# One score tensor of five banks for two heads, and a third bank for the other products, in a thresholded-attention and feed-forward kernel

## The chip, the cores and the metric

The kernel runs on one core of one Trainium2 chip. The metric is the time of the whole kernel on the device, in microseconds; before the change it is 1397.89 us (median of three runs, 1397.81 to 1398.3).

## What is computed

Two blocks follow each other, for a batch of 8 sequences of 576 tokens. The first is attention over 8 heads of 64 features, in which a weight is kept only where the score comes within tau of the row's largest score:

```python
scores = scale * np.matmul(q, k.transpose(0, 1, 3, 2))
thresh = np.max(scores, axis=-1, keepdims=True) - tau
scores = np.where(scores >= thresh, scores, -1000000000.0)
scores = scores - np.max(scores, axis=-1, keepdims=True)
attn = np.exp(scores)
attn = attn / (np.sum(attn, axis=-1, keepdims=True) + 1e-09)
return np.matmul(attn, v).astype(np.float32)
```

The heads' outputs are put side by side into rows x of 512 features. The second block normalizes each row and puts it through two layers with 2048 hidden features:

```python
xn = (x - mu) / np.sqrt(var + 1e-06) * g_ln
ch = np.maximum(xn @ w_ch1, 0.0) @ w_ch2
return (x + ch).astype(np.float32)
```

q, k, v and tau are fp32; the weights of the second block can come as 64-bit floats, and are then converted on the chip in the first part of the run.

## The kernel before

**Steps.** The work is cut into 72 steps, nine to a batch (`SLOTS`). A step handles a pair of heads and 256 query rows: steps 0 to 3 the first 256 rows of the four pairs of heads, steps 5 to 8 the second half's, and step 4 (`s == HP`) the 64 rows that are left over, of all pairs at once. Each step has four blocks of 128 rows by 576 scores, two to a head.

**Scores** (`scores`, L373 to L394). A head has 64 features, so its matmuls use 64 of TensorE's 128 rows; head 0 uses the upper half, head 1 the lower, and both run at the same time. Each head has a PSUM tensor of its own of three banks of 512 fp32 columns (L361). Its two blocks begin at column 128 (`FREE`) and end at 1280, and `span` (L366) cuts them at bank borders into pieces of 384, 192, 320 and 256 columns. The pieces are sorted so that the heads take turns. An fp32 matmul shows as two records in the profile, a pass each.

**What reads the scores.** `exponentials` (L396): VectorE takes the row maxima of a head's two blocks in one reduction (L404, one for each head), GpSimd makes the thresholds of them (L408), ScalarE takes the four exponentials (L415), two before the step's first quarter of other work and two after it. `weights` (L417): VectorE multiplies each block by its mask and sums the rows (L422), takes the reciprocals (L427, in batch 0 L429), and GpSimd divides (L438). In batch 0 the division is instead part of a product with a diagonal matrix.

**Weights times v.** The weights are turned, from batch 1 on by VectorE's block transposes (L504, L498) and a round trip through DRAM (scr, then em and rest, issued on SyncE's queue), in batch 0 by TensorE (`turn_weights`, tiles tp and tr). One step later `values_of` (L532) multiplies them by v (L550); ScalarE copies the result to x (L567, L558). Before the change the result lies in `pv_behind`: the 256 columns behind head 0's scores, in the same bank as the end of these scores. Only in steps 0 to 4 of batch 0 it takes a tile of the pool `ps_ff` instead.

**The other products.** Everything else on TensorE (tp and tr; the mean; p1, the first layer; var; p2 and seg, the second layer) takes one bank at a time of the pool `ps_ff`, which has two banks in turn (L76). ScalarE empties most of them (L472, L487, L729, L812), VectorE the mean, in the centring (L599). The second layer's products are done in seven segments, with sums and differences on VectorE and GpSimd (L797, L816, L824).

**Order.** Each engine runs its instructions in the order in which the program issues them. The loop at L949 issues a step: first its scores, then the reductions and the first two exponentials, then four quarters of other work: `second_part` deals out pieces of the two layers by a planned share, `turn` prepares the next q and k on VectorE (L341 to L351, in steps 8, 0, 1 and 2), small calls that have been put off run between, and at set quarters of the next step the turned weights are fetched and multiplied by v. In batch 0 and the start of batch 1, `conversion.tick()` puts the conversion of weights between, most of it on VectorE (L269 to L296). The framework itself adds the waits between engines, from what each instruction reads and writes.

Of the kernel before, what the change touches and what calls it, by code (L numbers as in the profile page):

```python
# [8 lines left out]
F32 = mybir.dt.float32  # L9
# [9 lines left out]
def kernel(  # L19
# [31 lines left out]
    nc = tc.nc  # L51
    B, H, S, D = q.shape
# [3 lines left out]
    HP = H // 2  # L56
# [5 lines left out]
    QH = 256  # L62
# [9 lines left out]
    small = ctx.enter_context(tc.tile_pool(name="small", bufs=4))  # L72
    dram = ctx.enter_context(tc.tile_pool(name="dram", bufs=3, space=bass.MemoryType.DRAM))
    ffn = ctx.enter_context(tc.tile_pool(name="ffn", bufs=2))
    ps_sc = ctx.enter_context(tc.tile_pool(name="ps_sc", bufs=1, space=bass.MemoryType.PSUM))
    ps_ff = ctx.enter_context(tc.tile_pool(name="ps_ff", bufs=2, space=bass.MemoryType.PSUM))  # L76

    tau_sb = consts.tile([128, 1], F32, name="tau_sb")
    scl_sb = consts.tile([128, 1], F32, name="scl_sb")
# [278 lines left out]


    FREE = 128  # L360
    sc = [ps_sc.tile([128, 3 * 512], F32, name=f"sc{i}") for i in range(2)]  # L361
    pv_behind = sc[0][:, FREE + 2 * S : FREE + 2 * S + QH]
    pairs = [t[:, FREE : FREE + 2 * S].rearrange("p (j n) -> p j n", j=2) for t in sc]
    blocks = [pairs[i // 2][:, i % 2] for i in range(4)]

    def span(at, n):  # L366

        while n:
            m = min(n, 512 - at % 512)
            yield at, m  # L370
            at, n = at + m, n - m

    def scores(b, s):  # L373


        hp, half = (s, 0) if s < HP else (s - HP - 1, 1)

        pieces = []
        for h in range(2):
            t = 0  # L380
            for j in range(2):
                first = FREE + j * S
                for at, n in span(first, S):
                    pieces.append((t, h, j, at, n, at - first))
                    t += n
        for t, h, j, at, n, o in sorted(pieces):
            r = slice(64 * h, 64 * h + 64)
            for i in range(2 if s == HP else 1):
                qT, kT, ql = turned[b * HP + (2 * j + i if s == HP else hp)]
                nc.tensor.matmul(  # L390
                    sc[h][64 * i : 64 * i + 64 if s == HP else 128, at : at + n],
                    lhsT=ql[r] if s == HP else qT[r, half, j * 128 : (j + 1) * 128],
                    rhs=kT[r, o : o + n], start=True, stop=True,
                )  # L394

    def exponentials(n):  # L396


        neg = small.tile([128, 4], F32, tag="neg", name="neg")
        thr = small.tile([128, 4], F32, tag="thr", name="thr")  # L400
        es = e_room[(n + 1) % 2 if n < SLOTS else 0]
        for h in range(2):
            i = slice(2 * h, 2 * h + 2)
            nc.vector.tensor_reduce(  # L404
                out=neg[:, i], in_=pairs[h],
                axis=AXL.X, op=ALU.max, negate=True,
            )
            nc.gpsimd.tensor_scalar(  # L408
                out=thr[:, i], in0=neg[:, i], scalar1=-1.0, scalar2=low_sb,
                op0=ALU.mult, op1=ALU.add,  # L410
            )
        for i in range(4):
            if i == 2:
                yield es, thr
            nc.scalar.activation(es[:, i], blocks[i], func=AF.Exp, bias=neg[:, i : i + 1])  # L415
# [111 lines left out]
    def x_of(g):  # L527
        if g not in groups:
            groups[g] = ffn.tile([128, NK, TOK], F32, tag="x", bufs=3, name="x")
        return groups[g]  # L530

    def values_of(b, s, turned_weights):  # L532

        em, er = turned_weights
        pv = pv_behind
        if b == 0 and s <= HP:
            pv = ps_ff.tile([128, QH], F32, tag="ff", name="pv")
        if s == HP:
            outs = [(hp, pv[:, hp * 64 : hp * 64 + 64]) for hp in range(HP)]
            pick = lambda t, hp, h: t[  # L540
                :, hp % 2 * 2 : hp % 2 * 2 + 2, (2 * h + hp // 2) * 32 : (2 * h + hp // 2) * 32 + 32
            ]
        else:
            outs = [(s if s < HP else s - HP - 1, pv)]
            pick = lambda t, hp, h: t[:, :, 64 * h : 64 * h + 64]
        for hp, dst in outs:
            vt, vr = values_in[b * HP + hp]
            for c in range(J + 1):
                for h in range(2):
                    nc.tensor.matmul(  # L550
                        dst[64 * h : 64 * h + 64],
                        lhsT=vt[:, h, c, :] if c < J else vr[:, h, :],
                        rhs=pick(em[:, :, c] if c < J else er, hp, h),
                        start=(c == 0), stop=(c == J),
                    )
        if s == HP:
            for t in range(2):
                nc.scalar.copy(  # L558
                    x_of(2 * b + t)[:, :, QH:],
                    pv.rearrange("p (u t x) -> p t u x", u=HP, t=2)[:, t],  # L560
                )
                for c in range(1, NK):
                    add_feature(2 * b + t, c, slice(QH, TOK))
        else:
            g = 2 * b + (s > HP)
            hp = outs[0][0]
            nc.scalar.copy(x_of(g)[:, hp, :QH], pv)  # L567
            if hp:
                add_feature(g, hp, slice(0, QH))

    def add_feature(g, c, cols):

        x = groups[g]
        if g not in sums:
            sums[g] = ffn.tile([128, TOK], F32, tag="sum", bufs=2, name="sum")
        nc.gpsimd.tensor_tensor(  # L576
            out=sums[g][:, cols], in0=x[:, 0, cols] if c == 1 else sums[g][:, cols],
            in1=x[:, c, cols], op=ALU.add,
        )
# [369 lines left out]
    for n in range(NS):  # L949
        b, s = divmod(n, SLOTS)  # L950
        ticks = (1, 3, 4)[: 2 + n // 3] if n < 6 else range(1, 7)

        def tick(i):
            if i in ticks:
                conversion.tick()

        scores(b, s)
        run(n, -1)
        rest = exponentials(n)
# [34 lines left out]
        else:  # L994
# [9 lines left out]
        at_quarter(  # L1004
            n + 1, 1 if b == 0 and s <= HP else 3,
            lambda b=b, s=s, box=box: values_of(b, s, box[0]),
        )
        if s in (HP, 2 * HP):
# [52 lines left out]
```

## Time and profile before

| | |
|---|---|
| median of three runs | 1397.89 us |
| the profiled execution | 1397.5 us |
| its span, first to last instruction | 1395.7 us |
| TensorE (PE) busy | 1337.3 us, 96% |
| VectorE (DVE) busy | 931.2 us, 67% |
| GpSimd (POOL) busy | 609.7 us, 44% |
| ScalarE (ACT) busy | 460.4 us, 33% |
| granted TensorE clock | 0.993 |
| one batch from the third on | 160.60 us |
| scores (L390), products with v (L550) on the chain that ended last | 10% and 10% of the span |

Times are in microseconds from the span's start. A row of the view in order of time gives the start, the length, the engine, the line, the operation, what it writes and reads, its shape, and how many instructions were merged in it; in brackets stands how long the engine had been idle, and which instruction it waited for. A row of the list of waits gives who waited for whom, the total, the number of times and the longest. Busy time of matmuls comes from modelled ends, so a busy TensorE is not TensorE at its peak.

### The profile page before, as it was taken

The page shows a single profiled execution, that of the slowest core. Times are in us where ns is not written, and L with a number is a line of the kernel's source. Part 1 is how long each engine was busy: PE and PEld are TensorE (multiplying, and loading weights), DVE is VectorE, ACT ScalarE, POOL GpSimd, SP SyncE. Part 2 cuts the span into 40 slices and gives each one's busy share as a digit, 9 for nine tenths or more (in the row PEclk, how much of TensorE's full clock was granted, in tenths as well). Part 3 has the DMA queues.
Part 4 walks back from the last instruction along what each step waited for, and adds up shares of the span by engine and source line. Part 5 has one row for each costly group of instructions (what it writes and reads, how often), then busy time and mean ns, then how long its engine had stood idle before and what let it go on. Part 6 is the DMA issues. An engine that isn't in the chain of part 4 may idle for free.

```text
span 1395.7 us, 35606 instructions
## 1 busy us (share of the span) xinstructions
PE 1337.3 (96%) x15048; PEld 986.9 (71%) x15048; DVE 931.2 (67%) x1638; ACT 460.4 (33%) x923; POOL 609.7 (44%) x809
## 2 busy tenths in 40 slices
PE   4888999999999999999999999999999999999996
PEld 3665665867768596877869586776858677685966
DVE  5998967676776767657776767657775767766211
ACT  3877613232332323232232323323232323323120
POOL 2444444544433454343444455353444444334413
PEclk8999999999999999999999999999999999999998
DMA  9722355447744476446754477445764476443211
GB/s 231 175 77 70 95 145 153 154 146 187 196 133 159 136 191 180 142 137 185 192 160 146 150 196 188 138 148 151 187 180 143 134 183 184 127 161 129 63 18 18
DMA packets 316383, 205.48 MB, mean 147 GB/s; under 512 B 242368, under 2 KB 273856, under 8 KB 308160
## 3 DMA queue, kind: packets, MB, share of 16 engines
q1 hardware_dynamic: 311456, 202.62, 50.8%
q8 instruction: 118, 1.93, 0.6%
q10 hardware_dynamic: 4736, 0.59, 0.4%
q14 instruction: 41, 0.34, 0.1%
q0 software_dynamic: 32, 0.00, 0.0%
HBM read 119.41 MB, written 83.76 MB: 146 GB/s over the span
## 4 chain that ended last, share of the span: by engine, by line
PE 89%; DVE 5%; ACT 2%; issue 1%; POOL 0%; POOLq 0%; DVEq 0%; ACTq 0%
PE p L101 36%; PE seg L101 30%; PE sc L550 10%; PE sc L390 10%; DVE e L422 1%; PE tp L101 1%; DVE neg L404 1%; PE var L101 0%; PE mean L101 0%; DVE w L269 0%; ACT e L415 0%; PE tr L478 0%; ACT part L812 0%; DVE hidden L296 0%; DVE w L296 0%
## 5 line engine op out<-in xcount | busy, mean ns | idle before, releaser
L101 PE MATMUL p<-xc,w 128*64 128x288 f32 x4096 | 518.1, 408 | 13.0 <-ACT hidden L729 5.5
L101 PEld LDWEIGHTS p<-xc,w 128*64 128x64 f32 x4096 | 288.9, 137 | 224.6 <-ACT hidden L729 16.0
L404 DVE TENSOR_REDUCE neg<-sc 128x2 f32<-128x1152 f32 x144 | 188.8, 1352 | 271.1 <-PE sc L390 271.0
L415 ACT ACTIVATE e<-sc,neg 128x576 f32<-128x576 f32 x288 | 196.8, 744 | 247.7 <-DVE neg L404 247.7
L438 POOL TENSOR_SCALAR e<-e,den 128x576 f32<-128x576 f32 x252 | 194.1, 783 | 134.5 <-DVE den L427 134.3
L101 PE MATMUL seg<-hidden,w 128*64 128x144 f32 x3840 | 248.0, 287 | 0.0
L101 PEld LDWEIGHTS seg<-hidden,w 128*64 128x64 f32 x3840 | 235.1, 137 | 11.6 <-issue 7.7
L422 DVE SCALAR_TENSOR_TENSOR e<-sc,thr,e 128x576 f32<-128x576 f32 x288 | 222.0, 810 | 13.9 <-ACT e L415 13.2
L729 ACT ACTIVATE hidden<-p 128x288 f32<-128x288 f32 x256 | 105.9, 414 | 241.0 <-PE p L101 239.2
L408 POOL TENSOR_SCALAR thr<-neg,low_sb 128x2 f32<-128x2 f32 x144 | 42.5, 295 | 306.1 <-DVE neg L404 302.1
L390 PE MATMUL sc<-kT,qT 64*128 64x384 f32 (+3 forms) x1024 | 150.6, 425 | 20.1 <-DVE qT L350 10.1
L504 DVE STREAM_TRANSPOSE et<-e 128x1152 f32<-128x1152 f32 x112 | 153.1, 1374 | 14.8 <-POOL e L438 14.0
L390 PEld LDWEIGHTS sc<-kT,qT 64*128 64x128 f32 x1024 | 94.3, 191 | 69.9 <-issue 18.2
L550 PE MATMUL sc<-em,v_in 128*64 128x256 f32 (+1 forms) x1408 | 130.8, 329 | 0.0
L101 PE MATMUL seg<-hidden,stage 128*64 128x144 f32 x1920 | 123.1, 286 | 0.0
L101 PEld LDWEIGHTS seg<-hidden,stage 128*64 128x64 f32 x1920 | 117.9, 137 | 3.5 <-issue 2.3
L550 PEld LDWEIGHTS sc<-em,v_in 128*64 128x64 f32 x1408 | 86.4, 137 | 32.2
L797 POOL TENSOR_TENSOR hidden<-hidden 128x576 f32<-128x576 f32 x60 | 84.4, 1426 | 27.3 <-ACT hidden L729 19.0
L576 POOL TENSOR_TENSOR sum<-sum,x 128x256 f32<-128x256 f32 (+1 forms) x64 | 32.6, 509 | 113.2 <-ACT x L567 110.7
L797 DVE TENSOR_TENSOR hidden<-hidden 128x576 f32<-128x576 f32 x60 | 49.1, 853 | 47.8 <-PE seg L101 38.1
L567 ACT COPY x<-sc 128x256 f32<-128x256 f32 x60 | 22.3, 372 | 164.7 <-PE sc L550 115.3
L812 ACT COPY part<-seg 128x288 f32<-128x288 f32 x75 | 30.1, 401 | 131.2 <-PE seg L101 109.6
(151 smaller groups left out, 1186.6 us busy)
## 6 DMA issues: line engine op xcount, KB each, us to landing
scr<-et SPq DMA_DIRECT2D x63, 1152.0 KB, 4.9
em<-scr SPq DMA_DIRECT2D x63, 1024.0 KB, 5.9
out_dram<-ot SPq DMA_DIRECT2D x256, 36.0 KB, 4.9
q_in<-in_q_dram SPq DMA_DIRECT2D x124, 72.0 KB, 2.7
k_in<-in_k_dram SPq DMA_DIRECT2D x120, 72.0 KB, 3.0
rest<-scr SPq DMA_DIRECT2D x63, 128.0 KB, 6.0
v_in<-in_v_dram SPq DMA_DIRECT2D x28, 256.0 KB, 5.2
w<-in_moe_w_ch_dram SPq DMA_DIRECT2D x10, 512.0 KB, 6.2
```

What stands on the lines that cost most here:

```text
L101: nc.tensor.matmul(out[r], lhsT=lhsT[:, r], rhs=rhs, **flags)
L390: nc.tensor.matmul(sc[h][64 * i : 64 * i + 64 if s == HP else 128, at : at + n], lhsT=ql[r] if s == HP else qT[r, half, j * 128 : (j + 1) ...
L404: nc.vector.tensor_reduce(out=neg[:, i], in_=pairs[h], axis=AXL.X, op=ALU.max, negate=True,)
L408: nc.gpsimd.tensor_scalar(out=thr[:, i], in0=neg[:, i], scalar1=-1.0, scalar2=low_sb, op0=ALU.mult, op1=ALU.add,)
L415: nc.scalar.activation(es[:, i], blocks[i], func=AF.Exp, bias=neg[:, i : i + 1])
L422: nc.vector.scalar_tensor_tensor(out=es[:, i], in0=blocks[i], scalar=thr[:, i : i + 1], in1=es[:, i], op0=ALU.is_ge, op1=ALU.mult, accum_o ...
L438: nc.gpsimd.tensor_scalar(out=es[:, i], in0=es[:, i], scalar1=den[:, i : i + 1], scalar2=1.0, op0=ALU.mult, op1=ALU.mult,)
L504: nc.vector.transpose(et[:, :, 64 * h : 64 * h + 64].rearrange("p n (j c) -> p j n c", j=2), es[:, 2 * h : 2 * h + 2].rearrange("p j (n c) ...
L550: nc.tensor.matmul(dst[64 * h : 64 * h + 64], lhsT=vt[:, h, c, :] if c < J else vr[:, h, :], rhs=pick(em[:, :, c] if c < J else er, hp, h) ...
L576: nc.gpsimd.tensor_tensor(out=sums[g][:, cols], in0=x[:, 0, cols] if c == 1 else sums[g][:, cols], in1=x[:, c, cols], op=ALU.add,)
L729: nc.scalar.activation(hidden[:, d], p1, func=AF.Relu)
L797: eng.tensor_tensor(out=out[at], in0=in0[at], in1=in1[at], op=op)
```

## The change

Both heads' scores go into one PSUM tensor of five banks. Head 0 keeps columns 128 to 1280; head 1 follows directly, from 1280 to 2432. The third bank (columns 1024 to 1536, `BOTH`) so holds the end of head 0's scores and the start of head 1's. Head 1's pieces are cut at other places than before: 256, 320, 192 and 384 columns. In the sorted order head 1's piece in the shared bank is the second to be issued, and head 0's is the last.

[...] Therefore, after head 1's piece, VectorE copies one column of it to a small tile (`mark`), and head 0's piece in the same bank is made to wait for that copy by hand.

The bank that becomes free goes to `ps_ff`, which now has three in turn, and the products with v always take one of these; `pv_behind` is gone.

```diff
-    ps_ff = ctx.enter_context(tc.tile_pool(name="ps_ff", bufs=2, space=bass.MemoryType.PSUM))
+    ps_ff = ctx.enter_context(tc.tile_pool(name="ps_ff", bufs=3, space=bass.MemoryType.PSUM))
...
-    sc = [ps_sc.tile([128, 3 * 512], F32, name=f"sc{i}") for i in range(2)]
-    pv_behind = sc[0][:, FREE + 2 * S : FREE + 2 * S + QH]
-    pairs = [t[:, FREE : FREE + 2 * S].rearrange("p (j n) -> p j n", j=2) for t in sc]
+    sc = ps_sc.tile([128, 5 * 512], F32, name="sc")
+    BOTH = (FREE + 2 * S) // 512
+    in_order = mybir.DependencyInfo(mybir.DependencyClass.Sync, mybir.DependencyReason.DATA)
+    starts = [FREE, FREE + 2 * S]
+    pairs = [sc[:, at : at + 2 * S].rearrange("p (j n) -> p j n", j=2) for at in starts]
...
-                first = FREE + j * S
+                first = starts[h] + j * S
...
-                nc.tensor.matmul(
-                    sc[h][64 * i : 64 * i + 64 if s == HP else 128, at : at + n],
+                mm = nc.tensor.matmul(
+                    sc[64 * i : 64 * i + 64 if s == HP else 128, at : at + n],
...
+                if h == 0 and at // 512 == BOTH:
+                    tc.add_manual_dep(mm.ins, seen.ins.name, in_order, reason="same bank")
+            if h == 1 and at // 512 == BOTH:
+                mark = small.tile([128, 1], F32, tag="mark", name="mark")
+                seen = nc.vector.tensor_copy(mark, sc[:, at : at + 1])
...
-        pv = pv_behind
-        if b == 0 and s <= HP:
-            pv = ps_ff.tile([128, QH], F32, tag="ff", name="pv")
+        pv = ps_ff.tile([128, QH], F32, tag="ff", name="pv")
```

## The prediction, made before the result was known

> **What bounds the kernel now.** I read the page first (busy shares, chain), then a table of one stretch per batch, the list of waits, and then instructions in order of time around two steps. TensorE is nearly always busy, and from 330 us on each batch of nine steps repeats the last one exactly; here are the busy shares of the page and, from the table by stretches, one such batch (length, then busy time of PE, PEld, DVE, ACT, POOL, granted clock, DMA share, GB/s):
>
> ```profile
> PE 1337.3 (96%) x15048; PEld 986.9 (71%) x15048; DVE 931.2 (67%) x1638; ACT 460.4 (33%) x923; POOL 609.7 (44%) x809
> ...
> 651.70:812.30 160.60, 159.97 (x1826) 118.43 (x1824) 109.37 (x195) 47.51 (x96) 72.46 (x101) 1.00 0.57 163
> ```
>
> PE is idle for 0.63 us of 160.60. So every microsecond that TensorE waits in these batches is a microsecond of the total, and hardly any wait is left to be won. The list of waits says what there is:
>
> ```profile
> DVE neg L404 <- PE sc L390: 271.0, 64, 7.6
> ACT e L415 <- DVE neg L404: 247.7, 65, 6.4
> ...
> PE sc L390 <- DVE e L422: 11.1, 9, 7.2
> ...
> PE p L101 <- ACT hidden L729: 5.5, 3, 2.8
> PE p L101 <- ACT part L812: 4.6, 8, 0.6
> ```
>
> VectorE waits for scores (271 us in 64 waits), and that is slack. TensorE's waits for a bank to be emptied by ScalarE (5.5 and 4.6 us, and in the first 100 us some 11.7 us of tp and tr for em) are all that a third bank can give back. One step in order of time (batch 4, step 3):
>
> ```profile
> 705.83 2.21 PE L390 MATMUL sc<-kT,qT 64*128 64x384 f32 x16
> ...
> 707.37 0.48 DVE L643 STREAM_TRANSPOSE ot<-y 128x288 f32<-128x288 f32 x1 [0.79 <-POOL y L816]
> ...
> 708.14 2.62 DVE L404 TENSOR_REDUCE neg<-sc 128x2 f32<-128x1152 f32 x2 [0.29 <-PE sc L390]
> 709.59 1.37 ACT L415 ACTIVATE e<-sc,neg 128x576 f32<-128x576 f32 x2 [3.23 <-DVE neg L404]
> ...
> 710.86 0.41 ACT L729 ACTIVATE hidden<-p 128x288 f32<-128x288 f32 x1
> ...
> 711.07 0.82 DVE L422 SCALAR_TENSOR_TENSOR e<-sc,thr,e 128x576 f32<-128x576 f32 x1 [0.31 <-ACT e L415]
> 711.15 1.38 ACT L415 ACTIVATE e<-sc,neg 128x576 f32<-128x576 f32 x2
> ```
>
> Call the start of the scores S (705.83). VectorE ends its earlier work 2.02 us after S; the reduces follow at S+2.31; ScalarE's first two exponentials start as soon as the first head's reduce is over, beside the second reduce; the first masking product (L422) needs two exponentials, not four.
>
> Two more places show how accesses to one PSUM tensor are ordered:
>
> ```profile
> 71.50 0.79 DVE L422 SCALAR_TENSOR_TENSOR e<-sc,thr,e 128x576 f32<-128x576 f32 x1
> ...
> 72.22 0.80 DVE L422 SCALAR_TENSOR_TENSOR e<-sc,thr,e 128x576 f32<-128x576 f32 x1
> ...
> 73.09 0.91 PE L390 MATMUL sc<-kT,qT 64*128 64x384 f32 x2 [0.42 <-DVE e L422]
> ...
> 687.17 0.37 ACT L567 COPY x<-sc 128x256 f32<-128x256 f32 x1 [5.43 <-DVE y L816]
> 687.80 1.81 PEld L390 LDWEIGHTS sc<-kT,qT 64*128 64x128 f32 x16 [0.20 <-ACT x L567]
> ```
>
> The first score piece goes to columns 128 to 512, bank 0 of the first tensor. At 73.09 it is released by the second masking product, which reads banks 1 and 2, not by the first, which reads bank 0 and ended 0.7 us before; at 687.80 by a copy out of bank 2. I take it that all accesses of different engines to one PSUM tensor run in the order of the program, whatever their banks. This is the choice that the forecast hangs on.
>
> [...]
>
> **The change, part by part.**
>
> *The mark, VectorE free.* The pieces now run head 0 (384 columns), head 1 (256, shared bank), the mark, then six more. The wait written out is for head 0's last piece only; by the order above already the third piece (head 1, 320) waits for the mark, since it writes the same tensor. Scores cost 0.83 ns per column and pass, two passes, the heads side by side: 2 x 1152 x 0.83 + 0.11 at the front = 2.04 us to the last column. Head 1's first piece is done at 0.11 + 2 x 0.21 + 0.17 (a 256-column record lasts 0.384 us, 0.21 of it columns) = 0.70. VectorE starts 0.10 later (reduce against the end of the scores, 705.83 + 2.21 to 708.14). The mark is not in the trace; the nearest row is a reciprocal of 128x2 at 0.166 us, with 0.08 (accumulator read, 128x1) and 0.30 as bounds: 0.17. To TensorE 0.05 (73.04 to 73.09). It resumes at 1.02; head 1 has 896 columns left, 1.49 + 0.11, so the end is 2.62 in place of 2.04: **+0.58 us a step**, bounds 0.4 to 0.9. All later matmuls queue behind it, so nothing covers it. The uneven pairs of pieces (up to 0.1 us) lie inside this.
>
> *The mark, VectorE late.* If VectorE ends its work P after S, the mark starts at P+0.06, TensorE resumes at P+0.28 and ends at P+1.88: the cost is P - 0.16. Last VectorE instruction against S in a steady batch, read as above for steps 0 to 8: -3.8, -3.4, -0.6, +2.0, -2.2, -1.4, -4.4, -5.2, +1.0.
>
> *The exponentials.* In one tensor the first exponential must wait for the second reduce: 1.3 us later. The first masking product must wait for the last exponential, not the second. In step 3 above: exponentials from 710.86, two until 712.2, the eviction of p until 712.6, two more until 713.9; masking starts at 713.95 and not 711.07: 2.9 later. Without an eviction between, 2.5. In step 2, where VectorE turns the next q and k meanwhile, 1.7; in step 1 nothing, as VectorE has other work until 678.22. POOL's divisions, the transposes and what follows on VectorE move with it (the waits between them are on each other). The em transfers move too, but they land 3.8 to 10 us before they are used in steps of this kind, so they stay hidden. So P becomes 2.0 + 1.7 at step 3, -1.4 + 2.7 at step 5, 1.0 + 2.5 at step 8.
>
> *Steady batch:* six steps at 0.58 = 3.5; step 3: 3.5; step 5: 1.2; step 8: 3.3; the centring that starts a group at step 6 (at 606.34 right behind the masking, first p at 607.78) comes 2.5 later, about 1.5 of it on TensorE. Sum 13.0, times six batches (2 to 7): **78**.
>
> *Batch 1:* steps at 165, 227, 261 and 313 us have P = 2.2, 4.9, 0.8, 1.0; with the shift 3.3 + 6.4 + 3.3 + 3.3, five at 0.58, centring 1.5: **21**.
>
> *Batch 0:* from 37 to 94 us VectorE converts weights and is itself the bound (its reduces start 3 to 6 us after the scores began). There each of five steps gains on VectorE the mark plus the wait for the remaining scores, 2.1 (P+2.1 to the reduce, where it followed at once before), and about 1.8 for the later exponentials: 19.5. Step 7: 0.6. Step 8 (142.41, VectorE busy until 148.45): 6.0 + 1.2 - 0.16 = 7.0. Sum **27**.
>
> *The third bank and v's products.* The two-bank waits: 5.5 of p goes; the 4.6 at the group starts is covered by the late centring; tp and tr lie where VectorE bounds. The scores' wait for the copy of v's products (1.2 us in 6 places) goes. **-7**, between 0 and -22 (all of them). v's products cost the same instructions as before; in the third bank they take the place that p or seg would have had, with as many banks between for those as before. This bank also covers the later evictions (up to 1.3 us behind the exponentials, against 1.9 us for a p group): without it that would be a further wait.
>
> Sum: 78 + 21 + 27 - 7 = 119. The profiled execution's span is 1395.7 us, its time 1397.5, the median of three runs 1397.89: 1397.5 + 119 = **1516 us**. Its own range is 1475 to 1560 (mark 0.08 to 0.30, shifts of masking 1.3 to 3.2, batch 0 from 15 to 35).
>
> **Rivals.**
>
> *Order by bank only.* Then only head 0's last piece waits, which starts 1.61 after S; with VectorE free the mark is done at 1.0 and costs nothing. Masking moves 0.6 (only the second exponential shares a bank with the second reduce). Steady: step 3 1.3, step 8 0.3, so 10; the start some 25; the bank -7: about 1425. For it: the wait was written out by hand, which it need not be under the wider order. Against it: the rows at 73.09 and 687.80.
>
> *Faster.* The waits for banks, at most 5.5 + 4.6 + 11.7 + 1.2 = 23, come back and the mark hides: 1388. It decides only if the mark costs below 0.1 us a step, that is under 7 us over 72. For it: VectorE is idle ahead of the reduces in 64 of 72 pairs. Against it: it is still busy at S+2.0 and S+1.0 in every batch, and 5 us past S in the first.
>
> *VectorE becomes the bound in every step,* by waits of its chain that I left at nothing (POOL, transposes): 21 us a step against 17.8 over 60 steps, about 1590. Against it: at steps 0, 1, 6 and 7 it has 3.4 to 5.2 us to spare.
>
> **How the numbers follow.** Chances: forecast 0.74, order by bank 0.13, faster 0.04, VectorE-bound 0.09. The range 1415 to 1580 holds nearly all of the first, half of the second and a third of the last. 0.2% is about what a measurement of this kernel can tell from no change; faster 0.05, within it 0.01, slower 0.94.
>
> **What would show it.** Right: matmuls of L390 waiting for the mark in all 72 steps, 0.3 to 0.5 us in most and 3 us or more at steps 3 and 8; the first exponential 2.7 us after the reduces start and the first masking product at 5.3 or later; a steady batch of 172 to 175 us. Wrong: batches near 161 to 163, exponentials beside the second reduce, or the third piece starting without a wait.

## The result, and the profile after

The changed kernel takes 1578.88 us (median of 4 runs, 1575.52 to 1580.43), the kernel before beside it 1397.85 us (4 runs): ratio 1.1293, 95% interval 1.1271 to 1.1314. It is 181 us slower. The forecast had said slower, 1516 us, with 1580 as the upper end of its range; its likeliest case, 1475 to 1560, was too small.

The page of the changed kernel (span 1578.4 us): busy shares, the granted clock in 40 slices, and the share of each engine on the chain that ended last.

```profile
PE 1417.3 (90%) x15048; PEld 1033.5 (65%) x15048; DVE 952.0 (60%) x1710; ACT 457.8 (29%) x923; POOL 607.5 (38%) x809
...
PEclk9779999999999999999999999998999999999998
...
PE 56%; DVE 23%; ACT 8%; POOL 5%; issue 4%; DMA 3%; SPq 0%; DVEq 0%; ACTq 0%; POOLq 0%
```

Two things are to be seen. TensorE's share falls from 96% to 90%: it stands. But its busy time also grows, from 1337.3 to 1417.3 us, with the same 15048 instructions. Not all of that is work: in step 2 of batch 4 below the sixteen score records count 0.91 + 1.77 us, where sixteen such records counted 2.21 us before. But part of the growth is a lower clock, which was in no part of the forecast. The row of the clock hardly shows it, as a slice is 39 us long; before, it began with 8999 and stayed at 9 up to the last slice's 8.

One batch (batch 4, from the start of its first scores to that of the next batch), in the columns of the table by stretches: length, busy time of PE, PEld, DVE, ACT and POOL, granted clock, DMA share, GB/s.

```profile
754.21:934.68 180.47, 168.67 (x1826) 121.92 (x1824) 112.69 (x204) 47.08 (x96) 72.61 (x101) 0.97 0.50 145
```

Before it was 160.60 us with 159.97 busy and a clock of 1.00. Now TensorE stands for 11.8 us and is busy for 8.7 us more.

The list of waits (who waits for whom; total, times, longest):

```profile
ACT e L422 <- DVE neg L411: 419.9, 65, 10.8
...
DVE neg L411 <- PE sc L392: 158.4, 71, 3.5
DVE mark L401 <- PE sc L392: 148.8, 44, 8.1
...
DVE e L429 <- ACT e L422: 126.0, 58, 3.5
...
PE sc L392 <- DVE mark L401: 89.1, 72, 7.3
...
PE p L101 <- DVE xc L604: 19.1, 8, 3.6
```

TensorE waits for the mark in all 72 steps. 28 times the mark itself had nothing to wait for: VectorE was late. The slack of the reduces (271.0 us before) is down to 158.4 us. The exponentials now wait longer for the reduces (247.7 us before). The wait for the centred x has grown to 19.1 us in 8 places (before 1.9 us in one).

In the costliest groups, the mark: count, busy time, mean length in ns, and what it waited for.

```profile
L401 DVE COPY mark<-sc 128x1 f32<-128x1 f32 x72 | 10.9, 152 | 148.8 <-PE sc L392 148.8
```

In order of time, the scores of step 2 of batch 4 on TensorE, where VectorE is free:

```profile
792.31 0.91 PE L392 MATMUL sc<-kT,qT 64*128 64x384 f32 x4
793.49 1.77 PE L392 MATMUL sc<-kT,qT 64*128 64x320 f32 x12 [0.27 <-DVE mark L401]
```

After four records (head 0's first piece and head 1's in the shared bank, two records each) all the other twelve wait, not head 0's last piece alone. And step 3 of the same batch, on all three engines:

```profile
811.08 0.91 PE L392 MATMUL sc<-kT,qT 64*128 64x384 f32 x4
...
814.00 0.48 DVE L648 STREAM_TRANSPOSE ot<-y 128x288 f32<-128x288 f32 x1 [0.78 <-POOL y L821]
814.40 0.12 DVE L401 COPY mark<-sc 128x1 f32<-128x1 f32 x1
...
814.58 2.66 PE L392 MATMUL sc<-kT,qT 64*128 64x320 f32 x12 [2.59 <-DVE mark L401]
...
817.29 2.62 DVE L411 TENSOR_REDUCE neg<-sc 128x2 f32<-128x1152 f32 x2 [2.77 <-PE sc L392]
...
820.03 1.37 ACT L422 ACTIVATE e<-sc,neg 128x576 f32<-128x576 f32 x2 [8.42 <-DVE neg L411]
...
823.06 0.82 DVE L429 SCALAR_TENSOR_TENSOR e<-sc,thr,e 128x576 f32<-128x576 f32 x1 [3.15 <-ACT e L422]
```

The mark stands behind a transpose of the second layer's output that was issued before it and waits for GpSimd; VectorE ends that work 3.40 us after the scores' start. TensorE stands for 2.59 us. The first exponential comes 2.74 us after the first reduce starts, the first masking product 5.77 us after it. The twelve score records that took 1.77 us in step 2 take 2.66 us here. The table by stretches shows why (the 0.74 us behind the stand, and two times 3.41 us):

```profile
814.57:815.31 0.74, 0.73 (x7) 0.71 (x9) 0.00 (x0) 0.00 (x0) 0.08 (x1) 1.00 1.05 382
815.31:818.72 3.41, 3.41 (x17) 1.62 (x15) 1.43 (x2) 0.00 (x0) 0.00 (x0) 0.50 0.84 238
818.72:822.13 3.41, 3.41 (x32) 1.98 (x30) 1.19 (x1) 2.10 (x4) 0.53 (x2) 1.00 0.00 0
```

0.74 us after the stand the granted clock falls to a half, for 3.41 us: 17 matmul records are under way in that stretch against 32 in the next. In the whole run such stretches sum to 152 us, of which TensorE is busy for 118 us; before it was 19 and 7 us. In the five whole steady batches there is one with every stand of 2.2 us or more (steps 3, 6 and 8; 15 of 15).

### The profile page after: what moved, and what is told of

Read it like the earlier page. It is cut to its first block, busy times and chain, and to the rows that moved or that the text cites. A ratio compares the mean times of both kernels' runs of the same rounds, so it can differ in the third digit from the quotient of the medians.

```text
span 1578.4 us, 35476 instructions
## 1 busy us (share of the span) xinstructions
PE 1417.3 (90%) x15048; PEld 1033.5 (65%) x15048; DVE 952.0 (60%) x1710; ACT 457.8 (29%) x923; POOL 607.5 (38%) x809
## 4 chain that ended last, share of the span: by engine, by line
PE 56%; DVE 23%; ACT 8%; POOL 5%; issue 4%; DMA 3%; SPq 0%; DVEq 0%; ACTq 0%; POOLq 0%
PE p L101 21%; PE seg L101 16%; PE sc L392 11%; DVE e L429 7%; ACT e L422 6%; PE pv L555 6%; DVE neg L411 5%; POOL e L445 3%; DVE et L511 2%; PE tp L101 2%; DMA v_rest<-in_v_dram 1%; DVE hidden L802 1%; DVE hidden L673 1%; POOL y L829 1%; POOL y L821 1%
## 5 line engine op out<-in xcount | busy, mean ns | idle before, releaser
L101 PE MATMUL p<-xc,w 128*64 128x288 f32 x4096 | 544.0, 422 | 21.2 <-DVE xc L604 19.1
L101 PEld LDWEIGHTS p<-xc,w 128*64 128x64 f32 x4096 | 314.2, 143 | 244.1 <-issue 70.5
L392 PE MATMUL sc<-kT,qT 64*128 64x320 f32 (+3 forms) x1024 | 199.3, 484 | 112.2 <-DVE mark L401 82.6
L411 DVE TENSOR_REDUCE neg<-sc 128x2 f32<-128x1152 f32 x144 | 188.8, 1352 | 158.4 <-PE sc L392 158.4
L101 PEld LDWEIGHTS seg<-hidden,w 128*64 128x64 f32 x3840 | 235.0, 137 | 19.0 <-issue 10.2
L392 PEld LDWEIGHTS sc<-kT,qT 64*128 64x128 f32 x1024 | 106.4, 209 | 175.7 <-DVE mark L401 123.6
L555 PE MATMUL pv<-em,v_in 128*64 128x256 f32 (+1 forms) x1536 | 143.3, 327 | 0.2
L555 PEld LDWEIGHTS pv<-em,v_in 128*64 128x64 f32 x1536 | 95.2, 137 | 34.5 <-ACT em L479 1.9
L401 DVE COPY mark<-sc 128x1 f32<-128x1 f32 x72 | 10.9, 152 | 148.8 <-PE sc L392 148.8
L802 DVE TENSOR_TENSOR hidden<-hidden 128x576 f32<-128x576 f32 x60 | 55.8, 965 | 45.7 <-PE seg L101 26.3
L572 ACT COPY x<-pv 128x256 f32<-128x256 f32 x64 | 23.8, 372 | 169.8 <-PE pv L555 169.8
```

What stands on the lines that cost most here:

```text
L101: nc.tensor.matmul(out[r], lhsT=lhsT[:, r], rhs=rhs, **flags)
L392: mm = nc.tensor.matmul(sc[64 * i : 64 * i + 64 if s == HP else 128, at : at + n], lhsT=ql[r] if s == HP else qT[r, half, j * 128 : (j + 1 ...
L411: nc.vector.tensor_reduce(out=neg[:, i], in_=pairs[h], axis=AXL.X, op=ALU.max, negate=True,)
L555: nc.tensor.matmul(dst[64 * h : 64 * h + 64], lhsT=vt[:, h, c, :] if c < J else vr[:, h, :], rhs=pick(em[:, :, c] if c < J else er, hp, h) ...
L802: eng.tensor_tensor(out=out[at], in0=in0[at], in1=in1[at], op=op)
```

## The experiments

A steady batch is one from the third to the seventh, in which the steps repeat; before, it takes 160.6 us. Lines are counted in each kernel for itself.

**The mark alone.** The kernel before, its two tensors kept; VectorE's copy after head 1's first piece (384 columns here), and head 0's last piece made to wait for it.

```diff
-                nc.tensor.matmul(
+                mm = nc.tensor.matmul(
...
+                if h == 0 and at == 1024:
+                    tc.add_manual_dep(mm.ins, seen.ins.name, in_order, reason="same bank")
+            if h == 1 and t == 0:
+                mark = small.tile([128, 1], F32, tag="mark", name="mark")
+                seen = nc.vector.tensor_copy(mark, sc[1][:, at : at + 1])
```

> The kernel before with its two score tensors, with the mark alone: VectorE copies one column of head 1's first piece, and head 0's last piece waits for it. Nothing of the exponentials, the third bank or the products with v is changed. My theory (strict order in one PSUM tensor makes the mark hold up the scores, the same order delays the exponentials and with them the mark of later steps, and waits of some 2 us or more bring TensorE down to half its clock): 0.6 us in each step with VectorE free, 1.9 in step 3 and 0.8 in step 8 of a batch, so a steady batch of 167 to 168.5 us instead of 160.6, full clock in the steady batches, total 1465 to 1495. Rival, the mark is the whole cost: total about 1579, a steady batch of 181.

Measured: 1470.63 us, ratio 1.0518 (1.0503 to 1.0534); a steady batch 166.0 us; 0.55 us more in a step where VectorE is free. The time and the full clock (1.00 over batch 4) are as expected; the batch is 1 us below, as step 3 cost 1.4 us and not 1.9. The second part of the scores of this kernel's step 3 (batch 4), on TensorE in order of time:

```profile
758.73 1.56 PE L391 MATMUL sc<-kT,qT 64*128 64x192 f32 x10 [0.78 <-DVE mark L400]
```

Even here ten of sixteen records wait, not the last piece's two: the mark reads head 1's tensor, and so head 1's later pieces come after it. The order by whole tensors holds here too, in the old layout.

**The later exponentials alone.** The kernel before, with the first exponential made to wait for the second reduce, and the first masking product for the last exponential.

```diff
-            nc.scalar.activation(es[:, i], blocks[i], func=AF.Exp, bias=neg[:, i : i + 1])
+            ex = nc.scalar.activation(es[:, i], blocks[i], func=AF.Exp, bias=neg[:, i : i + 1])
+            if i == 0:
+                tc.add_manual_dep(ex.ins, red.ins.name, in_order, reason="order")
+        last_exp[0] = ex
...
+            if i == 0:
+                tc.add_manual_dep(masked.ins, last_exp[0].ins.name, in_order, reason="order")
```

> The kernel before with the order of the exponentials alone: the first exponential waits for the second head's reduction, the first masking product for the last exponential, both by waits written out. No mark, no third bank. My theory: TensorE does not wait for VectorE in the scores, so only the centring at step 6 comes through (some 2 us, and 1 to 2 more where the clock drops), and the start of batch 0: a steady batch of 162 to 165 us, total 1410 to 1445. Rival, the late exponentials alone starve TensorE of banks or operands: above 1470.

Measured: 1466.44 us, ratio 1.0496 (1.0477 to 1.0514); a steady batch 168.0 us. Slower than expected. Two lines of this kernel's list of waits say where a good part of it goes:

```profile
PE p L101 <- ACT hidden L737: 29.9, 31, 2.8
PE p L101 <- DVE xc L607: 17.0, 8, 3.3
```

The late exponentials make ScalarE's evictions of p late, and two banks cannot cover that: 29.9 us of waits against 5.5 before. The prediction had named this wait and left it out because the changed kernel has a third bank. The second line is the centring, which was expected. Together they grew by some 40 of the 69 us; the rest was not taken apart.

**Both together.** The two edits above in one kernel, still in the old layout.

```diff
+                seen = nc.vector.tensor_copy(mark, sc[1][:, at : at + 1])
...
+                tc.add_manual_dep(ex.ins, red.ins.name, in_order, reason="order")
...
+                tc.add_manual_dep(masked.ins, last_exp[0].ins.name, in_order, reason="order")
```

> The kernel before with the mark and the order of the exponentials together, still with three banks for each head, two for the other products, and the products with v behind the scores. My theory: the two add up to more than their sum, since the late exponentials make VectorE late for the mark; VectorE ends 3.4 us after the scores' start in step 3 and 4.4 in step 8, a steady batch is 179 to 183 us, and the total is 1570 to 1605, the changed kernel's time plus what its third bank gives. Rival, the products with v in the ring of banks cost much of the time: clearly below 1560.

Measured: 1547.39 us, ratio 1.1068 (1.1051 to 1.1084); steady batches 174.5 to 175.9 us. The expectation was missed: the sum of the two alone is 73 + 69 = 142 us, both together cost 150, so they add nearly simply, and 31 us to the changed kernel are left. At step 3 VectorE ends its work 2.7 us after the scores' start, at step 8 3.5 (changed kernel: 3.4 and 4.4).

**The remaining waits of one tensor.** As the last kernel, and all pieces after the mark wait for it, and the first reduce waits for the last score piece of both heads.

```diff
-                if h == 0 and at == 1024:
+                last_mm[0] = mm
+                if held[0] is not None:
+                    tc.add_manual_dep(mm.ins, held[0].ins.name, in_order, reason="same bank")
+                    held[0] = None
...
+                held[0] = nc.vector.tensor_copy(mark, sc[1][:, at : at + 1])
...
+            if h == 0:
+                tc.add_manual_dep(red.ins, last_mm[0].ins.name, in_order, reason="order")
```

> The kernel before with its two tensors of three banks and two other banks, the mark and the later exponentials as in the run before it, and two further waits that one tensor brings: every score piece issued after the mark waits for it (not head 0's last piece alone), and the first reduce waits for the last score piece of both heads. Nothing of the computation is changed. If these two are what parts the changed kernel from the run with mark and order (1579 against 1547): 1565 to 1590, a steady batch of 178 to 182 us, the work of VectorE ending at least 0.5 us later after the scores' start at steps 3 and 8 than in that run. If the gap lies in the third bank, the products with v or the uneven cut: 1543 to 1556, a steady batch of 174 to 176.

Measured: 1567.04 us, ratio 1.1212 (1.1196 to 1.1229); steady batches 176.3 to 179.5 us. The time is in the range of the first case, so these two waits are worth 20 of the 31 us. The reason given was wrong in one part: VectorE's end at steps 3 and 8 did not move (2.7 and 3.5 us). The loss is 0.4 us in most steps, and there the scores do not end later (last record at 2.4 us in both kernels); the first reduce starts 0.36 us later (2.91 us after the scores' start against 2.55), all that follows moves with it, and TensorE's wait for evictions of p grows from 8.2 to 15.9 us. Behind a late mark two more records are still to come, as head 0's second piece waits too: the gap in step 3 of batch 4 grows from 1.58 to 1.89 us. To the changed kernel 12 us are left; what still differs is the third bank, the products with v in the ring, and the cut of the pieces.

**Two banks.** The changed kernel with `ps_ff` at two banks.

```diff
-    ps_ff = ctx.enter_context(tc.tile_pool(name="ps_ff", bufs=3, space=bass.MemoryType.PSUM))
+    ps_ff = ctx.enter_context(tc.tile_pool(name="ps_ff", bufs=2, space=bass.MemoryType.PSUM))
```

> The changed kernel with two banks in the ring instead of three, the products with v still in it. Nothing of the computation is changed. By the prediction's remark that the third bank covers the later evictions: 1590 to 1640, with matmuls of p and of the transposes that wait for ScalarE by more than 20 us in sum. If the third bank is worth nothing here: 1574 to 1585.

Measured: 1587.87 us, ratio 1.1361 (1.1344 to 1.1378), between the two expectations. The third bank is worth 9 us in the changed kernel. Two lines of the list of waits, with two banks:

```profile
PE sc L392 <- DVE mark L401: 70.1, 72, 5.1
...
PE p L101 <- ACT hidden L734: 14.0, 23, 2.8
```

With three banks the second wait is 2.1 us, but the first is 89.1: the bank takes waits away from TensorE, which then comes to the scores earlier, finds VectorE still at work (at step 3 it ends 3.40 us after the scores' start, with two banks 2.70), and gives the time back at the mark. Against the kernel with all the waits in the old layout, a layout whose two banks must hold the products with v too, and with the other cut, costs 21 us (1587.87 against 1567.04), of which the third bank returns 9.

**The mark on ScalarE.** The changed kernel, with the copy made by ScalarE. It still reads the score tensor.

```diff
-                seen = nc.vector.tensor_copy(mark, sc[:, at : at + 1])
+                seen = nc.scalar.copy(mark, sc[:, at : at + 1])
```

> The changed kernel with the mark taken by ScalarE instead of VectorE, all else as it is. ScalarE has emptied its last bank half a microsecond after the scores begin, so its mark is never late. My theory: the 0.65 to 0.75 us of each step stay, the waits of 3 to 4 us in steps 3 and 8 go with their clock drops, the centring of step 6 stays: a steady batch of 169 to 172 us, total 1465 to 1500. Rival, the clock drops come from the many short waits and not from the long ones: 1520 or more, with three half-clock stretches a batch as before.

Measured: 1494.47 us, ratio 1.0694 (1.0677 to 1.071); steady batches 169.4 to 171.1 us. As expected: 84 us of the loss is VectorE's lateness at the mark, with what hangs on it. In step 3 of batch 4 the wait is 0.27 us, as in steps where VectorE is free, though VectorE is as late as before (its earlier work ends 3.5 us after the scores' start):

```profile
766.43 1.77 PE L392 MATMUL sc<-kT,qT 64*128 64x320 f32 x12 [0.27 <-ACT mark L401]
```

Over this step, with its short wait, the granted clock is 1.00. Over batch 4 (171.10 us) it is 0.99, as much as one stretch of 3.41 us at half clock makes.

**A guard that does not read the scores, on VectorE.** The copy takes a constant from SBUF and waits, by a dependency written out, for head 1's piece.

```diff
-                seen = nc.vector.tensor_copy(mark, sc[:, at : at + 1])
+                seen = nc.vector.tensor_copy(mark, eps_sb)
+                tc.add_manual_dep(seen.ins, mm.ins.name, in_order, reason="piece done")
```

> The changed kernel, but the mark copies a constant that lies in SBUF, on VectorE, and waits for head 1's first piece by a dependency written out; so it is no access to the score tensor, and only head 0's last piece waits for it. The result is as before. If the wait of the third piece for the mark is what costs in most steps: scores end 1.8 to 1.9 us after they start where VectorE is free (2.5 with the mark as it is), a steady batch of 166 to 172, a time of 1490 to 1530. If the ordering of the exponentials alone makes the loss: 1550 or more.

Measured: 1489.47 us, ratio 1.0656 (1.064 to 1.0672), just below the range; steady batches 168.0 to 171.4 us. Where VectorE is free the last score record starts 1.83 us after the first, as in the kernel before (2.47 in the changed one): the guard is hidden there. In step 3, where VectorE is late, fourteen records run and only the last piece's two wait:

```profile
762.68 2.21 PE L392 MATMUL sc<-kT,qT 64*128 64x384 f32 x14
...
766.20 0.70 PE L392 MATMUL sc<-kT,qT 64*128 64x256 f32 x2 [1.30 <-DVE mark L401]
```

So it is the read of the score tensor that holds the other pieces, not the written-out wait.

**The same guard on ScalarE.**

```diff
-                seen = nc.vector.tensor_copy(mark, sc[:, at : at + 1])
+                seen = nc.scalar.copy(mark, eps_sb)
+                tc.add_manual_dep(seen.ins, mm.ins.name, in_order, reason="piece done")
```

> The changed kernel, but the guard for the shared bank is a copy of a constant in SBUF on ScalarE that waits for head 1's first piece; it is no access to the score tensor and stands in no long queue. What is left of the change is the later exponentials, reduces that wait for both heads, and the third bank. The result is as before. From the run with the mark on ScalarE (1494, scores 0.64 us longer in each of 72 steps) less 72 x 0.64 = 46: 1435 to 1460, a steady batch of 163 to 166, scores that end 1.8 to 1.9 us after they start in all steps. If the two banks of the run with the order alone did not matter: 1462 to 1470, as there.

Measured: 1442.12 us, ratio 1.0314 (1.0297 to 1.0331); steady batches mostly 164.1 us. As expected. Scores run through at step 3 (all sixteen records in 2.21 us). 44 us of the loss are left. On TensorE's list of waits stand the centred x (19.3 us), evictions of p by ScalarE (12.3 us, although there are three banks) and, in five places, the mark (10.2 us). Next to the run that has the order alone on two banks (1466.44) this suggests that the third bank can return some 20 us where no mark takes them back; it is not shown, as that run also differs in the cut of the pieces, in the place of the products with v and in the wait of the first reduce. The four runs on the guard, in one view:

| the copy | reads the scores | reads a constant |
|---|---|---|
| on VectorE | 1578.88 (the change) | 1489.47 |
| on ScalarE | 1494.47 | 1442.12 |

**Work in the stands.** The changed kernel computes all it did, and besides 5 products of 288 columns at step 3 and 7 at step 8 of batches 2 to 7, behind the second score piece, which nobody uses.

```diff
+                if b > 1 and s in FILL:
+                    idle = ps_ff.tile([128, TOK], F32, tag="ff", name="idle")
+                    for k in range(FILL[s]):
+                        product(idle, lhsT=avg_sb, rhs=w1_sb[0][:, :TOK], start=k == 0, stop=k == FILL[s] - 1)
```

> The changed kernel, and in batches 2 to 7, at steps 3 and 8 behind the second score piece, 5 and 7 products of 288 columns that nobody uses, in a bank of the ring, so that TensorE is at work where it stood. It computes everything as before and some products more. If the clock that falls to half after a stand of over 2 us costs 2 to 2.5 us a time: 12 such stretches are gone, the granted clock is over 0.965, and the time is 1545 to 1565 in spite of the added work. If the lower clock costs nothing (work then waits for others anyway): 1579 or more.

Measured: 1555.81 us, ratio 1.1124 (1.1106 to 1.1143); steady batches mostly 177.4 us. More work, and 23 us less time. Then the same with 3 more such products before the first product of p at step 6 (`FILL` as above):

```diff
+            if d == 0 and g >= 4 and g % 2 == 0:
+                idle = ps_ff.tile([128, TOK], F32, tag="ff", name="idle")
+                for k in range(3):
+                    product(idle, lhsT=avg_sb, rhs=w1_sb[0][:, :TOK], start=k == 0, stop=k == 2)
```

> The kernel with added products in the stands of steps 3 and 8 and, besides, 3 such products in front of the first product of p at step 6, where TensorE stands for 2.2 us until the centred x is there (batches 2 to 7). It computes everything as before and some products more. If this stand trips the clock too: no stretch of half clock is left in the steady batches, a batch of 175.5 to 176.5 us, a time of 1540 to 1552. If it does not matter: 1554 to 1560, with batches of 177.4.

Measured: 1548.28 us, ratio 1.1072 (1.1056 to 1.1089); steady batches 175.7 us, 5.1 us under the changed kernel's mean. Batch 4 in the table by stretches, where the clock is at 1.00 (0.97 in the changed kernel), and its step 3 in order of time; over the whole run the clock is 0.972 (0.952):

```profile
741.88:917.61 175.73, 171.28 (x1887) 124.31 (x1885) 112.60 (x204) 47.12 (x96) 73.02 (x101) 1.00 0.51 149
```

```profile
798.74 0.91 PE L393 MATMUL sc<-kT,qT 64*128 64x384 f32 x4
799.58 2.65 PE L101 MATMUL idle<-w,avg_sb 128*64 128x288 f32 x20
...
802.10 0.12 DVE L402 COPY mark<-sc 128x1 f32<-128x1 f32 x1
...
802.28 1.77 PE L393 MATMUL sc<-kT,qT 64*128 64x320 f32 x12
```

The mark comes at the same place (3.36 us after the scores' start, 3.32 without the added products), TensorE works until then, and the twelve score records behind it take 1.77 us and not 2.66. The lower clock with the stands of the steady batches is thus worth some 1578.88 - 1548.28 = 31 us, the price of the added products not counted.

## Why the prediction was right, and where its size was wrong

**Right: the order by whole tensors, and the waits that follow from it.** The choice on which the forecast hung, read from two rows of the kernel before, held: all pieces after the mark wait for it, in 72 of 72 steps; the first exponential comes 2.74 us after the reduces start (forecast 2.7), the first masking product at 5.77 in step 3 (forecast 5.3 or later). The rival of an order by bank only is refuted, as is "faster". VectorE as the bound of every step is too, though the time lies nearer to the 1590 us written for it than to 1516: its busy share fell to 60%, it waits 158 us for scores and 149 us for the shared piece, and it was late for the mark in 28 of 72 steps (2 to 8 in batch 0, then 3, 5 and 8).

**Luck: that the time lies in the range.** It does so by 1 us. The forecast's own range ended at 1560; the room above that was there for the case in which VectorE bounds every step, and a lower clock had no part in it. A steady batch of 172 to 175 us had been written down as a sign, and 180.5 to 181.3 came.

The forecast by its own terms, in microseconds; by stretches from the first reduce of one batch to that of the next, after less before:

| term | forecast | measured |
|---|---|---|
| six steady batches | 78 | 120 |
| batch 1 | 21 | 23 |
| batch 0, with the 1 us ahead of it | 27 | 39 |
| third bank | -7 | inside the others |
| tail (in no term) | 0 | 0 |
| sum (spans) | 119 | 183 |

**Wrong: the price of a stand, its length and nothing more.** This is the largest miss. The step "the cost is P - 0.16" counted only the time in which TensorE stands. With each stand of 2.19 us or more in the steady batches (15 of 15) a stretch of 3.41 us at a clock of 0.50 comes on top. If TensorE is busy throughout, half of it is lost, an estimate of 1.7 us; three of them make 5.1 us, and filling the stands gave back 5.1 us a batch, 31 us in all. The trace before does not show this price: its clock falls only in a stand of 7.25 us that begins at 14.3 us, and at the end of the run, while nine other stands of 1.0 to 2.75 us pass at full clock. Its batch 1, in the columns of the table by stretches, has 5.6 us of stands and a clock of 1.00:

```profile
165.40:330.50 165.10, 159.48 (x1638) 111.49 (x1636) 114.99 (x204) 48.99 (x97) 78.47 (x103) 1.00 0.50 147
```

**The steps of batch 4,** after less before, beside the same with the stands filled (clock at 1.00 throughout):

| steps | forecast | after | stands filled |
|---|---|---|---|
| 0, 1, 2, 4, 7 together | 2.9 | 4.0 | 4.2 |
| 3 | 3.5 | 4.5 | 2.9 |
| 5 | 1.2 | 1.7 | 1.6 |
| 6 | 2.1 | 4.0 | 2.4 |
| 8 | 3.3 | 5.8 | 4.1 |
| sum | 13.0 | 19.9 | 15.1 |

Without the clock the step costs stand within 1 us of the forecast, at steps 3 and 6 within 0.7. With the ends of VectorE that were measured (3.40, 1.96 and 4.42 us after the scores' start), P - 0.16 gives 3.2, 1.8 and 4.3 us at steps 3, 5 and 8, against 2.9, 1.6 and 4.1 with the stands filled: within 0.4 us, so without the clock the term holds. The mark with VectorE free was 0.64 us (last score record at 2.47 against 1.83; forecast 0.58, where the 2.04 us in its sum come to 2.02).

Step 8 was under-sized: VectorE ended 4.42 us after the scores' start, not 3.5. The masking of step 7 moved by 2.5 us as forecast (from 3.30 to 5.77 us after the first reduce), but the reduces themselves start 0.7 us later against the scores' start (3.00 against 2.31), which the shift left out. The third bank has its part too: with two banks VectorE ends just as long after the start of step 7's scores (21.74 us in both kernels), but TensorE comes to step 8's scores 0.96 us later (18.27 against 17.31 us), and the end lies 3.47 us after them. The forecast counted only the waits that the bank takes away, not that TensorE then meets a VectorE that is later for the mark. At step 3 the end was forecast at 3.7 and came at 3.40 (2.70 with two banks); the stand was 2.59 us where "3 us or more" was written.

**Batch 0.** The five steps where VectorE is the bound (2 to 6) cost 21.1 us (forecast 19.5). Missed were steps 0 and 1, which the forecast left at nothing and which cost 3.6 and 1.2 us; step 7, 2.7 (0.6); step 8, 9.9 (7.0). How much of these is the clock, which stands at a half for 51 us of the first 207, was not taken apart.

**Batch 1** came out near its forecast by compensation: step 5 cost 0.8 us and not 3.3, the first step took 1.1 us less than before where 3.3 more were forecast, and steps 6 and 8 cost 6.5 each and not 2.1 and 3.3.

**The third bank.** -7 is near the 9 us that taking it away cost. But the reasoning was that waits go and nothing comes back. In truth the bank removes waits in front of p (14.0 to 2.1 us) and lengthens those at the mark (70.1 to 89.1). Together with v's products, which share the ring, and the other cut of the pieces, it leaves the changed kernel 12 us slower than the old layout with all the waits added (1578.88 against 1567.04), so that as a whole this part of the change lost where the forecast had it gain. Which of the three makes these 12 us was not separated.

## What to carry to other kernels

Two buffers in one tensor had one order here (the pieces behind the mark waited for it in 72 of 72 steps): before joining buffers, list every reader and writer of both, and price each new wait, also those on pieces that have nothing to do with the shared bank. A guard should neither touch the tensor that it guards nor stand in the queue of an engine that runs late; here these two choices were worth 137 us (1578.88 against 1442.12), and no form of the guard brought the layout under 1397.85. That the shared bank needs a guard at all was not shown: no run leaves it out. Where the granted clock falls with a stand of TensorE, price the stand above its length (here by an estimated 1.7 us, half of 3.41 us at a clock of 0.50, at 15 of 15 stands of 2.19 to 3.65 us in the steady batches), and remember that a wait removed upstream makes TensorE earlier at the next one (here 0.96 us at step 8).

## What the runs showed of the hardware that was not expected

The granted clock falls to a half for 3.41 us, in the steady batches of the changed kernel 0.7 to 1.3 us after a stand ends; in two places it fell 1.7 us before the end of the stand, and then for 6.83 us. The changes do not come at one distance from the stands, but in each of the two traces, of the kernel before (3 changes) and of the changed one (57), all lie on one grid of 3.413 us, within 0.02 us.

The length of a stand alone does not tell whether the clock falls. In the five whole steady batches of the changed kernel 15 of 15 stands of 2.19 to 3.65 us came with a fall and none of five of 1.2 us. But in its batch 1 two stands of 2.32 us (at 238.1 and 301.9 us) passed at full clock, and so did one of 2.75 us at 109.3 us in the kernel before. With two banks TensorE stands for 13.4 us in batch 4, 2.4 us of them in step 3, at a clock of 1.00. With the guard on VectorE it stands for only 1.3 us in step 3 of batch 4, and the clock of that step is 0.92.

Most of this is a matter of how much of a stand falls into one interval of the grid. In the two traces, with the modelled ends of matmuls, TensorE was idle for more than 2.03 us in sum in 24 of the intervals at full clock, and half clock followed each of them. It followed none of the 758 with less than 1.17 us, and 5 of the 22 between; what decides there stays open. The stand of 3.64 us at step 8 of batch 4 leaves 1.53 us idle in one interval, after which the clock stayed, and 2.11 us in the next, after which it fell.

A copy of 128x1 out of PSUM took 0.152 us on VectorE in the mean of 72, close to the 0.17 that the forecast took, and TensorE resumed 0.06 us after its end (814.40 + 0.12 to 814.58).
